# A fused attention and maxout kernel: new order of the work ahead of its main loop, eleven zero products in place of twenty-seven, and the next batch's scores ahead of the first product in each iteration

## The chip, the core and the metric

The kernel runs on one core of one Trainium2 chip. Such a core has four engines that compute, each with an instruction queue of its own: TensorE (PE in the profile; its weight loads are PEld), VectorE (DVE), ScalarE (ACT) and GpSimd (POOL). A fifth, SyncE (SP), here only issues data transfers. Products are accumulated in PSUM, which this kernel holds as eight named banks of 128 x 512 float32. The time of a run is the time of the whole execution on the device, in microseconds (us).

## The reference

For each of 8 batches and 8 heads, `x` (512 x 64) reads from a small `state` (32 x 64), and the state reads from `x`. The two results are put together to 4352 tokens of 512 numbers, which go through a maxout layer of two weight matrices and an output matrix:

```python
scores = scale * np.matmul(x, state.transpose(0, 1, 3, 2))
a = np.exp(scores - scores.max(-1, keepdims=True))
a /= a.sum(-1, keepdims=True) + 1e-09
xread = np.matmul(a, state)                      # (8, 8, 512, 64)
# sread: the same with x and state exchanged       (8, 8, 32, 64)
x2 = np.concatenate([xread, sread], axis=2)      # heads merged: (4352, 512)
h1, h2 = x2 @ w1, x2 @ w2                        # 512 x 1024 each
out = np.maximum(h1, h2) @ w_out                 # 1024 x 512
```

## The kernel before

**Algebra.** max(h1, h2) is written as relu(h1 - h2) + h2. So the weights needed are `wd` = w1 - w2 (the `sub` pieces) and `wwo` = w2 @ w_out (the `ww` pieces, from transposed w2 in `w2m` and from `wo`, the bfloat16 copy of w_out). Since xread = a @ state, each batch b first multiplies its state with these weights (`sw` pieces, into the tile `sw`), and layer one is then relu of the transposed attention weights `at` times `sw` (`l1`, evacuated by `re` into the tile `r`). The output product of `r` with `wo` is made by a seven-product scheme in place of eight (Strassen's, as Winograd has it): products 1 to 7 (`p1` to `p7`, line 426, 8 matmuls of 256 columns each), sums of `r` (`rs`, `r_sum`, into `big5`), sums of `wo` (`wt`, into `big3`), parts kept on the way (`k0` to `k2`), `wwo`'s share added with line 432 (`p2o`, `o7`, `o3`, `o4`), and results put into the output tile (`v00` to `v10`).

**Stages.** Ahead of the loop, batches 0 and 1 are worked through entirely and batch 2 up to its attention weights, while the weights arrive. A loop over batches b = 2 to 6 then does layer one and the output products of batch b together with the scores, exponentials and state products of batch n = b + 1. A tail finishes batch 7 and the 256 tokens of the state's readings.

**What sets the order.** A manual schedule is used: every engine runs its instructions in the order in which the program calls them, and waits on semaphores for what it reads. Ahead of the loop that order is the string `ORDER` (lines 23 to 48), a list of pieces. `sc.2.0@4` is the first half of the scores of batch 2, into bank 4; `xte.0.1>V` is the copy of a transposed half of `x`, on DVE (A is ACT, P is POOL); `ld...` pieces are loads on SP, in the order of the list. The pieces that the prediction names:

- `fill.k@r`: one product of zeros (tile `wz`, line 575), of 512 columns (256 where k is below 100). Nothing reads it.
- `ldw2.k`, `ldw1.k`, `ldwo.k`: quarters of the weights, 512 KB each; `ldx.b.g`: half of a batch's `x`, 512 KB. `cw2`, `cwo`: casts of weights to bfloat16; `sub.k.h`: w1 - w2.
- `ce`, `cb`: casts of `x`; `xt`, `xte`: transposed `x` by TensorE, and its copy from PSUM; `xtd`: the same as a transposing transfer (line 242, tile `xt`).
- `sc`, `exp`, `red`, `mul`, `at`, `ate`: scores, exponential, sums, normalisation, transposed attention weights; `srw`, `swre`, `srp`, `sr`: the state's reading.
- `mS` (line 222), then `Sd` (line 228): the states of batches 2 to 7 are masked into the tile `sb`, and one transposing transfer makes the tile `sbd` of it. Scores from batch 2 on read `sbd`.

SP issues transfers in order, and a transfer waits in SP's queue until what it reads is written. Loads go through one queue, and each waits for the landing of the eighth transfer ahead of it.

In the loop, DVE runs `r_sum` 0 and 1, then the sums and reciprocals (`red`) of both score halves, then `r_sum` 2; POOL multiplies (`mul`) behind each `red`.

Of the kernel before, what the change touches and what calls it, by code (L numbers as in the profile page):

```python
# [24 lines left out]
fill.9@0 ldw2.3 fill.111@1 ldwo.2 fill.0@0 fill.5@1 fill.101@0 ldw1.3 ce.0.1>A ce.0.0>V ldwo.3 xt.0.0@0 cS.0.2>V  # L25
ldw1.2 fill.106@1 xte.0.0>V fill.105@2 ce.0.3>P ce.0.2>A ldw2.1 S.0.2@1 xt.0.1@2 ldw2.0 Se.0.2.1>A Se.0.2.0>V sc.0.0@1
xte.0.1>V fill.13@0 ldwo.0 fill.6@3 ce.1.2>P exp.0.0>A fill.115@4 fill.108@3 sc.0.1@4 ce.1.3>V ldwo.1 red.0.0>V
exp.0.1>A xt.1.1@3 ce.1.0>A ce.1.1>P srw.0@4,1 xte.1.1>V ldw1.0 mul.0.0>P swre.0.0>A red.0.1>V sc.1.1@3 xt.1.0@2
cw2.2>P exp.1.1>A ldw1.1 fill.15@4 fill.107@0 xte.1.0>V fill.1@4 swre.0.1>A fill.2@3 fill.14@0 fill.3@4 fill.112@3
cw2.3>A red.1.1>V mul.0.1>P fill.102@4 fill.7@3 ldx.2.0 fill.4@2 mul.1.1>V w2.3@2 cwo.2>A w2.2@3 w2e.3>V sc.1.0@4  # L30
at.0.0@0 at.0.1@1 exp.1.0>A w2e.2>V ww.3.2@2 ldx.2.1 ww.2.2@4 red.1.0>V sub.3.1>P ate.0.0>A srw.1@3,5 ate.0.1>A
mul.1.0>V cwo.3>A ww.0.2@1 sub.3.0>V at.1.0@0 at.1.1@6 swre.1.0>A ww.1.2@7 sub.2.0>V ate.1.1>A ldS.2.8 ww.3.3@2
ww.1.3@7 sub.2.1>V ate.1.0>A ww.0.3@1 swre.1.1>A sw.1.1@0,6 sw.0.1@5,3 swe.1.1.0>A swe.1.1.1>V ww.2.3@4 swe.0.1.0>A
swe.0.1.1>V l1.1.5@6 cw2.1>P srp.0>P srp.1>P l1.1.7@0 cw2.0>A re.1.5>V l1.0.7@3 w2.1@5 re.1.7>V re.0.7>A w2.0@6 w2e.1>V cwo.0>A
l1.0.5@3 l1.1.6@0 w2e.0>V l1.1.4@5 cwo.1>A ww.2.0@4 re.0.5>V ww.1.0@7 re.1.4>A ww.2.1@4 sub.0.0>V ww.1.1@7 re.1.6>A
sub.0.1>V ww.3.0@2 wwe.2>A ww.0.1@1 sub.1.1>V ww.3.1@2 wwe.1>A ww.0.0@1 sub.1.0>V wwe.3>A l1.0.4@7 wwe.0>A cb.2.0>P
sw.0.0@2,4 re.0.4>V wt.0>P sw.1.0@0,5 swe.0.0.0>A swe.0.0.1>V sw.0.w@1,3 sw.1.w@7,6 cb.2.1>P swe.1.0.0>A swe.1.0.1>V xtd.2 wt.1>P
p2.1@2 l1.0.6@4 swe.0.w.0>A re.0.6>V l1.0.3@0 l1.0.2@5 swe.0.w.1>A re.0.3>V swe.1.w.0>V mS.1>A
l1.0.1@4 l1.0.0@1 p2.0@3 swe.1.w.1>V mS.0>A Sd dif.0>P re.0.2>V re.0.1>A re.0.0>A p2o.0
l1.1.0@7 l1.1.1@6 l1.1.2@0 l1.1.3@5 re.1.0>V re.1.1>A re.1.2>A rs.0.0>V rs.0.1>V re.1.3>A  # L40
p2o.1 ldx.4.1 ldx.3.0 ldx.4.0 ldx.3.1
p1.0@1 k0.0>A p1.1@4 rs.0.2>V wt.2>V v00.0 p6.0 rs.0.3>V k0.1>A k1.0>A p5.0@7 wt.3>V v00.1 rs.1.0>V k2.0>A
sc.2.0@6 exp.2.0>A sc.2.1@0 exp.2.1>A sw.2.0@5,3 red.2.0>V mul.2.0>P red.2.1>V swe.2.0.0>A swe.2.0.1>A ce.2.0>A ce.2.1>A ce.2.2>A ce.2.3>A
p7.0 o7.0 v11.0 rs.1.1>V mul.2.1>P p3.0 o3.0 rs.1.2>V atd.2 sw.2.w@6,2 swe.2.w.0>A v01.0 swe.2.w.1>A
# [13 lines left out]
def kernel(  # L58
# [216 lines left out]
    def red(b, hh):  # L275
        nc.vector.tensor_reduce(es_all[:, b, hh], e_view(e_s[b % 2], hh), axis=AXX, op=ALU.add)  # L276
        nc.vector.reciprocal(er_s[b % 2][:, hh], es_all[:, b, hh])  # L277
# [145 lines left out]
    def product(pv, lhs, rhs, first=False, cc=(0, 1)):  # L423
        for c in cc:
            for f in range(4):
                nc.tensor.matmul(pv[c], lhs[:, f, 128 * c:128 * c + 128], rhs[:, f, :],  # L426
                                 start=first and f == 0 and (c == 0 or pv.split), stop=False, skip_group_check=True)
# [474 lines left out]
```

## Time and profile before

| | |
|---|---|
| time, median of 3 runs (lowest to highest) | 144.81 us (144.69 to 145.2) |
| the profiled execution: time, span of the profile | 144.88 us, 143.1 us |
| granted TensorE clock, mean | 0.996 |
| first zero product to first product of the loop | 1.29 us to 52.56 us |
| the five iterations | 52.7 to 119.5 us |
| HBM read, written | 15.20 MB, 8.91 MB |

The span covers the program's own instructions; 1.78 us of the execution lie around it. Each line of a timeline is a run of like instructions on one engine: start, length, engine and line of the code, operation, tile written and tiles read, shape, and in brackets how long the engine was idle before it and what ended that. A line number is often that of a helper (L102 is every copy on ACT), so the tiles tell what it is.

### The profile page before, as it was taken

The page shows a single profiled execution, that of the slowest core. Times are in us where ns is not written, and L with a number is a line of the kernel's source. Part 1 is how long each engine was busy: PE and PEld are TensorE (multiplying, and loading weights), DVE is VectorE, ACT ScalarE, POOL GpSimd, SP SyncE. Part 2 cuts the span into 40 slices and gives each one's busy share as a digit, 9 for nine tenths or more (in the row PEclk, how much of TensorE's full clock was granted, in tenths as well). Part 3 has the DMA queues.
Part 4 walks back from the last instruction along what each step waited for, and adds up shares of the span by engine and source line. Part 5 has one row for each costly group of instructions (what it writes and reads, how often), then busy time and mean ns, then how long its engine had stood idle before and what let it go on. Part 6 is the DMA issues. An engine that isn't in the chain of part 4 may idle for free.

```text
span 143.1 us, 3680 instructions
## 1 busy us (share of the span) xinstructions
PE 134.7 (94%) x1448; PEld 95.4 (67%) x1458; DVE 108.3 (76%) x197; ACT 86.9 (61%) x168; POOL 72.1 (50%) x99
## 2 busy tenths in 40 slices
PE   6889989999999999999999999999999999999980
PEld 2467725456787776786778477747876786788860
DVE  3488959868999938997899799669948997847420
ACT  4367589895689535855682769086726855753220
POOL 4147326099009993399269908971990464200000
PEclk9999999999999999999999999999999999999998
DMA  3999999945997979949995999759137042502073
GB/s 112 342 366 392 384 386 386 343 83 93 196 343 230 286 180 249 236 42 293 242 386 109 212 355 195 160 213 211 35 65 293 2 58 82 234 5 73 9 248 119
DMA packets 36452, 29.50 MB, mean 206 GB/s; under 512 B 22608, under 2 KB 32336, under 8 KB 35536
## 3 DMA queue, kind: packets, MB, share of 16 engines
q1 hardware_dynamic: 36160, 29.10, 70.8%
q8 instruction: 12, 0.20, 0.6%
q10 hardware_dynamic: 272, 0.13, 0.3%
q14 instruction: 8, 0.07, 0.1%
HBM read 15.20 MB, written 8.91 MB: 169 GB/s over the span
## 4 chain that ended last, share of the span: by engine, by line
PE 83%; DMA 11%; ACT 1%; issue 1%; DVE 0%; SPq 0%; DVEq 0%
PE bank L426 36%; PE bank L375 19%; PE bank L432 10%; DMA big<-in_moe_w_out_dram 8%; PE bank L352 5%; DMA big<-in_x_dram 4%; PE bank L606 3%; PE bank L473 2%; PE bank L515 2%; PE bank L264 2%; PE bank L304 2%; PE bank L513 1%; ACT wo L102 1%; PE bank L548 1%; PE bank L336 0%
## 5 line engine op out<-in xcount | busy, mean ns | idle before, releaser
L102 ACT COPY big<-bank 128x512 f32<-128x512 f32 (+2 forms) x40 | 21.9, 551 | 16.6 <-PE bank L426 8.4
L280 POOL TENSOR_TENSOR a<-e,er 128x512 bf16<-128x512 bf16 x14 | 16.7, 1209 | 29.5 <-ACT e L272 18.0
L370 DVE TENSOR_SCALAR r<-bank 128x512 bf16<-128x512 f32 x32 | 21.9, 690 | 11.7 <-PE bank L375 10.6
L375 PE MATMUL bank<-at,sw 128*128 128x512 bf16 x120 | 29.1, 379 | 0.6 <-DVE sw L104 0.2
L426 PEld LDWEIGHTS <-big 128*128 128x128 bf16 x256 | 23.9, 98 | 6.3 <-DVE er L277 2.1
L426 PE MATMUL bank<-big,big 128*128 128x256 bf16 x192 | 23.1, 273 | 0.1
L102 ACT CAST sw<-bank 128x512 bf16<-128x512 f32 x36 | 20.1, 608 | 3.2 <-PE bank L352 3.2
L375 PEld LDWEIGHTS <-sw 128*128 128x128 bf16 x128 | 12.2, 98 | 13.5 <-ACT sw L102 0.5
L368 ACT ACTIVATE r<-bank 128x512 bf16<-128x512 f32 x32 | 18.3, 597 | 4.9 <-PE bank L375 4.7
L426 PEld LDWEIGHTS <-r 128*128 128x128 bf16 x192 | 18.2, 98 | 3.8 <-issue 0.5
L402 DVE TENSOR_TENSOR big<-bank,big 128x512 f32<-128x512 f32 (+1 forms) x25 | 16.4, 660 | 5.4 <-PE bank L432 5.4
L106 POOL CAST xe<-big 128x512 bf16<-128x512 f32 x23 | 16.5, 749 | 6.1 <-DMA big<-in_x_dram 6.1
L426 PE MATMUL bank<-wo,r 128*128 128x256 bf16 x128 | 16.3, 273 | 0.0
L102 ACT COPY sread_t<-bank 128x128 bf16<-128x128 bf16 x8 | 3.2, 472 | 18.7 <-PE bank L336 15.5
L106 POOL CAST xb<-big 128x1024 bf16<-128x1024 f32 x12 | 12.2, 1035 | 4.7 <-DMA big<-in_x_dram 4.7
L432 PE MATMUL bank<-sw,at 128*128 128x256 bf16 x96 | 14.4, 273 | 0.0
L432 PEld LDWEIGHTS <-at 128*128 128x128 bf16 x128 | 12.5, 98 | 1.7
L402 DVE TENSOR_TENSOR big<-r 128x1024 bf16<-128x1024 bf16 x16 | 12.6, 788 | 0.6
L276 DVE TENSOR_REDUCE sums<-e 128x16 f32<-128x512 bf16 x16 | 10.6, 660 | 0.3 <-ACT e L272 0.2
L272 ACT ACTIVATE e<-bank 128x512 bf16<-128x512 f32 x16 | 8.9, 601 | 1.3 <-PE bank L264 1.3
L402 POOL TENSOR_TENSOR big<-sw 128x512 bf16<-128x512 bf16 x8 | 9.2, 1151 | 0.9 <-POOL a L280 0.9
L104 DVE CAST sw<-bank 128x512 bf16<-128x512 f32 x12 | 7.9, 679 | 0.6 <-PE bank L352 0.6
(100 smaller groups left out, 188.7 us busy)
## 6 DMA issues: line engine op xcount, KB each, us to landing
big<-in_x_dram SPq DMA_DIRECT2D x14, 512.0 KB, 6.2
out_dram<-big SPq DMA_DIRECT2D x7, 1024.0 KB, 5.3
big<-in_moe_w_dram SPq DMA_DIRECT2D x8, 512.0 KB, 12.0
big<-in_moe_w_out_dram SPq DMA_DIRECT2D x4, 512.0 KB, 11.6
big<-in_x_dram SPq DMA_DIRECT2D x1, 1024.0 KB, 6.9
out_dram<-big SPq DMA_DIRECT2D x4, 256.0 KB, 2.6
sf<-in_state_dram SPq DMA_DIRECT2D x1, 384.0 KB, 10.4
out_dram<-w2m SPq DMA_DIRECT2D x2, 128.0 KB, 2.5
```

Source lines behind the costliest of these rows:

```text
L102: nc.scalar.copy(o, i)
L104: nc.vector.tensor_copy(o, i)
L106: nc.gpsimd.tensor_copy(o, i)
L272: nc.scalar.activation(out=e_view(e_s[b % 2], hh).rearrange("p (g c) i n -> p g c (i n)", g=2), in_=p.rearrange("p (c g m) -> p g c m", c= ...
L276: nc.vector.tensor_reduce(es_all[:, b, hh], e_view(e_s[b % 2], hh), axis=AXX, op=ALU.add)
L280: (nc.gpsimd if eng == "P" else nc.vector).tensor_mul(e_view(a_s[b % 2], hh), e_view(e_s[b % 2], hh), er_s[b % 2][:, hh].unsqueeze(3).to_b ...
L368: nc.scalar.activation(out=o, in_=p, func=ACTF.Relu)
L370: nc.vector.tensor_scalar(o, p, scalar1=0.0, scalar2=None, op0=ALU.max)
L375: nc.tensor.matmul(p, sw_s[b % 3][:, g, f * 128:(f + 1) * 128], at_s[b % 3][:, g].rearrange("p c t -> p (c t)"), start=(g == 0), stop=(g = ...
L402: (nc.gpsimd if eng == "P" else nc.vector).tensor_tensor(o, i0, i1, op=op)
L426: nc.tensor.matmul(pv[c], lhs[:, f, 128 * c:128 * c + 128], rhs[:, f, :], start=first and f == 0 and (c == 0 or pv.split), stop=False, ski ...
L432: nc.tensor.matmul(pv[c], at_s[b % 3][:, g, 2 * i + c, :], rhs[:, g, :], start=False, stop=False, skip_group_check=True)
```

## The change

`ORDER` is replaced. It has the same pieces, except that 11 `fill` pieces, all of 512 columns and all at the very start, stand in place of 27 (of 256 and 512 columns) that were spread over the first stage. The engines of many copies, the banks, and the order on every engine differ. In the loop, the scores of batch n and their exponentials now come ahead of the first product, and `red` and `mul` of the two halves come between the sums:

```diff
 ORDER = """
-ldx.0.0 ldS.0.2 fill.10@0 ldx.0.1 fill.109@1 ldx.1.1 fill.114@0 fill.11@1 ldx.1.0 fill.110@0 ldw2.2 fill.100@1
...
+fill.101@4 fill.102@1 fill.106@0 fill.107@2 fill.103@3 fill.108@2 fill.110@4 fill.109@3 fill.105@4 fill.104@3
+fill.100@7 ldx.0.0 ldS.0.2 ce.0.1>A cS.0.2>V ce.0.0>V ldx.0.1 ce.0.3>P ldx.1.1 ldx.1.0 ce.1.2>P ce.1.1>P ldw2.2 ldw2.3
...
         pX, pY, pZ = Pair(BX), Pair(BY), Pair(BZ)
+        pp = [sc_mm(n, hh) for hh in range(2)]
+        for hh in range(2):
+            sc_ev(pp[hh], n, hh)
         product(pX, rq(b, 0, 0), wq(0, 0), True)
         keep(0, pX, "A")
         r_sum(b, 0, "V")
+        red(n, 0)
+        mul(n, 0, "P")
         r_sum(b, 1, "V")
-        pp = [sc_mm(n, hh) for hh in range(2)]
-        for hh in range(2):
-            sc_ev(pp[hh], n, hh)
         product(pZ, rq(b, 0, 1), wq(1, 0), True)
         opened(b, pZ, 0, so_half(b, 0))
         pg = [sw_mm(n, 512 * z, 512 * z + 512, BY if z == 0 else "r") for z in range(3)]
         sw_ev(pg[0], n, 0, 512, 0, "A")
         sw_ev(pg[0], n, 0, 512, 1, "A")
-        for hh in range(2):
-            red(n, hh)
-            mul(n, hh, "P")
+        red(n, 1)
+        mul(n, 1, "P")
         at_dma(n)
```

Three places in the engines' queues matter below. Lines of the changed kernel are lower by three in these rows.

**TensorE, near the 256th instruction of its program.** Of the kernel before, six rows (`a` feeds the transposed attention weights, `wo,w2m` is a `ww` product):

```order
L291 LDWEIGHTS a_93
L291 MATMUL bank_64<-ident_71,a_93 128x128
L606 LDWEIGHTS w2m_80
L606 MATMUL bank_65<-wo_77,w2m_80 128x512
L606 LDWEIGHTS w2m_80
L606 MATMUL bank_67<-wo_77,w2m_80 128x512
```

Of the changed kernel, at the same count of instructions:

```order
L288 MATMUL bank_69<-ident_71,a_93 128x128
L288 LDWEIGHTS a_94
L288 MATMUL bank_68<-ident_71,a_94 128x128
L603 LDWEIGHTS w2m_80
L603 MATMUL bank_64<-wo_77,w2m_80 128x512
```

Before, the 257th instruction was the first load of `ww.3.2`, the first of the `ww` products. Now it lies inside the transposes `at.1.0`, which come behind three `ww` products, and 32 instructions of zero products less stand ahead of it.

**SP's queue, behind the last weights.** Before (`sf` is the state, `xt0` and `sbd0` the transposing transfers `xtd.2` and `Sd`, `big1` and `big9` hold `x` of batches 4 and 3):

```order
L192 DMA sf0_81<-in_state_dram 128x12x64
L242 DMA_TRANSPOSE xt0_87<-xb0_89 128x16x128
L228 DMA_TRANSPOSE sbd0_74<-sb0_82 128x12x128
L167 DMA big1_110<-in_x_dram 128x4x256
L167 DMA big9_118<-in_x_dram 128x4x256
```

And now:

```order
L189 DMA sf0_81<-in_state_dram 128x12x64
L164 DMA big1_110<-in_x_dram 128x4x256
L164 DMA big9_118<-in_x_dram 128x4x256
L239 DMA_TRANSPOSE xt0_87<-xb0_89 128x16x128
L225 DMA_TRANSPOSE sbd0_74<-sb0_82 128x12x128
```

Two loads of `x` went ahead of the two transposing transfers. One mask piece that `sbd0` waits for, `mS.0`, also stands elsewhere, in ACT's queue. Before, both mask pieces followed the copies of `sw`:

```order
L102 CAST sw0_102<-bank3_66 128x512
L222 ACTIVATE sb0_82<-sf0_81,mask0_83 128x12x64 x2
L368 ACTIVATE r0_105<-bank4_67 128x512
```

Now six copies of layer one stand between the last copy of `sw` and `mS.0` (`mS.1` is on DVE):

```order
L99 CAST sw1_103<-bank5_68 128x512
L365 ACTIVATE r0_105<-bank7_70 128x512
L365 ACTIVATE r0_105<-bank0_63 128x512
L365 ACTIVATE r0_105<-bank6_69 128x512
L365 ACTIVATE r0_105<-bank7_70 128x512
L365 ACTIVATE r0_105<-bank5_68 128x512
L365 ACTIVATE r1_106<-bank1_64 128x512
L219 ACTIVATE sb0_82<-sf0_81,mask0_83 128x12x64
```

**DVE in the loop's first iteration.** Before (`big5` receives `r_sum`, `e1` holds the exponentials):

```order
L402 TENSOR_TENSOR big5_114<-r0_105 128x1024
L402 TENSOR_TENSOR big5_114<-big5_114,r0_105 128x1024
L276 TENSOR_REDUCE sums0_79<-e1_92 128x16
L277 RECIPROCAL er1_96<-sums0_79 128x16
L276 TENSOR_REDUCE sums0_79<-e1_92 128x16
```

And now:

```order
L399 TENSOR_TENSOR big5_114<-r0_105 128x1024
L273 TENSOR_REDUCE sums0_79<-e1_92 128x16
L274 RECIPROCAL er1_96<-sums0_79 128x16
L399 TENSOR_TENSOR big5_114<-big5_114,r0_105 128x1024
L273 TENSOR_REDUCE sums0_79<-e1_92 128x16
```

The second sum, which the product behind the `sw` pieces reads, moved behind one sum of exponentials and its reciprocal.

More of the change, by code (lines that the diff above doesn't have):

```diff
@@ L23 @@
 ORDER = """
-ldx.0.0 ldS.0.2 fill.10@0 ldx.0.1 fill.109@1 ldx.1.1 fill.114@0 fill.11@1 ldx.1.0 fill.110@0 ldw2.2 fill.100@1
[L25 to L44, printed above, removed]
@@ new lines @@
+xte.0.1>V ldwo.0 sc.0.1@5 ldwo.1 exp.0.0>A exp.0.1>A ce.1.3>V xt.1.1@0 srw.0@2,3 ce.1.0>A red.0.0>V xt.1.0@5 xte.1.1>A
+sc.1.1@0 swre.0.1>A swre.0.0>A exp.1.1>A red.0.1>V mul.0.1>V xte.1.0>V ldw1.0 mul.0.0>P at.0.0@7 red.1.1>V ate.0.0>V
+sc.1.0@4 exp.1.0>A red.1.0>V mul.1.0>V ldw1.1 cw2.2>P w2.2@6 srw.1@1,5 swre.1.1>V cw2.3>P w2.3@2 w2e.3>V w2e.2>A
+swre.1.0>A sub.3.0>V sub.3.1>V ldx.2.0 cwo.2>P ww.0.2@1 ww.1.2@7 mul.1.1>P ww.2.2@4 at.0.1@6 at.1.0@5 cwo.3>A ww.0.3@1
+ate.0.1>A ate.1.0>A at.1.1@0 ate.1.1>A srp.0>A ww.1.3@7 cw2.1>P cw2.0>P ldx.2.1 ldS.2.8 sub.2.1>V ww.3.2@2 sub.2.0>V
@@ new lines @@
+sw.1.1@0,6 sw.0.1@5,3 swe.1.1.0>A swe.0.1.1>A ww.3.3@2 ww.2.3@4 swe.1.1.1>V l1.1.7@6 re.1.7>A swe.0.1.0>V l1.0.5@0
+l1.0.7@5 re.0.5>V re.0.7>A cwo.0>P l1.1.6@6 re.1.6>A w2.1@3 w2e.1>V cwo.1>V wt.0>V w2.0@0 w2e.0>A srp.1>A l1.1.4@6
+l1.1.5@3 re.1.5>A re.1.4>A ww.2.0@4 ww.3.0@2 ww.1.0@7 ww.1.1@7 wwe.1>A ww.2.1@4 wwe.2>A ww.0.0@1 ww.3.1@2 wwe.3>A
+ww.0.1@1 cb.2.0>P sub.0.1>V sub.0.0>V l1.0.4@6 wwe.0>A sub.1.0>V sub.1.1>V ldx.4.1 sw.0.0@2,4 sw.1.0@0,5 sw.0.w@1,3
+re.0.4>V swe.0.0.0>A sw.1.w@7,6 swe.1.w.0>V swe.0.w.0>V swe.1.w.1>V swe.0.w.1>V cb.2.1>V wt.1>V p2.1@2 swe.1.0.0>A
@@ new lines @@
+swe.0.0.1>A swe.1.0.1>A l1.0.3@7 l1.0.0@0 re.0.3>A l1.1.3@1 l1.0.6@6 re.0.0>A ldx.3.0 re.0.6>A l1.0.1@7 re.0.1>A
+l1.0.2@5 re.0.2>A dif.0>V mS.1>V rs.0.0>V rs.0.2>V rs.0.1>V wt.3>V p2.0@4 re.1.3>A mS.0>A p1.0@0 l1.1.0@5 p2o.0 p2o.1
+k0.0>A ce.2.0>A v00.0 l1.1.2@3 re.1.2>A l1.1.1@6 re.1.1>A p6.0 k1.0>A re.1.0>A xtd.2 Sd p5.0@1 sc.2.0@4 k2.0>A
+rs.1.0>V exp.2.0>A red.2.0>V wt.2>P rs.0.3>P p7.0 o7.0 sc.2.1@7 v11.0 exp.2.1>A red.2.1>V p1.1@4 p3.0 k0.1>A rs.1.1>V
+v00.1 p4.0 o4.0 o3.0 v01.0 rs.1.2>V rs.1.3>V ce.3.0>P ce.2.2>P ce.3.1>P mul.2.0>P ce.2.1>P ce.2.3>P mul.2.1>P cb.3.0>P
```

7 lines of the change are left out of this document (4 added, 3 removed).

## The prediction

> **What bounds the kernel now.** First the page's busy times and its chain of waits, by engine:
>
> ```profile
> PE 134.7 (94%) x1448; PEld 95.4 (67%) x1458; DVE 108.3 (76%) x197; ACT 86.9 (61%) x168; POOL 72.1 (50%) x99
> PE 83%; DMA 11%; ACT 1%; issue 1%; DVE 0%; SPq 0%; DVEq 0%
> ```
>
> TensorE ends last, behind a stretch of transfers. Where each holds is told by the table of windows (length, PE busy, granted clock, DMA share, GB/s):
>
> ```profile
> 6.00:16.00 10.00, 8.44 (x112) 1.00 1.05 376
> 18.90:29.10 10.20, 9.97 (x69) 1.00 1.08 364
> 29.10:40.70 11.60, 11.47 (x109) 1.00 0.73 144
> 40.70:52.70 12.00, 12.00 (x163) 1.00 0.82 252
> 66.10:79.60 13.50, 13.44 (x164) 1.00 0.87 248
> ```
>
> Up to 16 us the transfers are full and PE partly multiplies zeros. From 18.9 us on PE is full: idle are 0.23, 0.13 and nothing in the next three windows, 0.06 in an iteration. So an end can come earlier only if real products move into the time before 18.9 us, or if PE's dense stretch starts earlier; any new wait behind it is paid in full. In the loop there is nothing to win on PE.
>
> **Term 1, the weights' arrival.** What waits for weights, and PE's first products behind them (`sw` and layer one):
>
> ```profile
> 13.75 1.04 ACT L102 CAST wo<-big 128x1024 bf16<-128x1024 f32 x1 [0.30 <-DMA big<-in_moe_w_out_dram]
> 15.16 1.27 POOL L560 TENSOR_TENSOR wd<-big,big 128x512 bf16<-128x512 f32 x1 [1.73 <-DMA big<-in_moe_w_dram]
> 17.81 1.04 ACT L102 CAST wo<-big 128x1024 bf16<-128x1024 f32 x1 [1.41 <-DMA big<-in_moe_w_out_dram]
> 18.99 1.29 DVE L560 TENSOR_TENSOR wd<-big,big 128x512 bf16<-128x512 f32 x2 [1.22 <-DMA big<-in_moe_w_dram]
> 20.29 0.67 PE L352 MATMUL bank<-wd,sbd 64*32 64x512 bf16 x16
> 21.66 1.46 PE L375 MATMUL bank<-at,sw 128*128 128x512 bf16 x6 [0.17 <-DVE sw L104]
> ```
>
> Consecutive loads of 512 KB are used at 13.75, 15.16, 17.81 and 18.99 us: steps of 1.4, 2.65 and 1.2 where 524 KB at 386 GB/s need 1.36. `wo.3` came about 1.3 us late. One packet stands there that is no data:
>
> ```profile
> 0.00:15.50 15.50, 12.65 (x128) 8.40 (x130) 9.98 (x22) 8.76 (x16) 6.75 (x27) 1.00 0.90 309
> ...
> q8 instruction: 1, 0.02, 65.4%
> ...
> q8 instruction: 12, 0.20, 0.6%
> ```
>
> The first row counts 128 + 130 = 258 PE instructions up to 15.5 us; the second is queue 8 in the tenth of a microsecond behind; the last is that queue over the span: 12 packets for 2906 PE instructions, one in 242, 0.2 MB / 12 = 16 KB each. So I read it as the fetch of PE's next 256 instructions: one of the 16 DMA engines is taken for about a transfer's step, and the load that needs all sixteen lands late. The change takes 32 instructions out ahead of this place, so the 257th is reached in `at.1.0`, at about 17.5 us by the sums below, and `wo.3` should land at 15.1 + 1.36 = 16.45 and `w1.2` at 17.8 us. Loads behind stay 1.2 late as before.
>
> [...]
>
> **Term 2, PE up to the first `sw`.** The early stage itself is gated by the loads of `x`: both orders have the first reading products (`srw.0`) at about 10.1 us, since the same casts and exponentials lie ahead. From there DVE leads. Its pieces in the new order, by durations of like rows (copy of 1024 from PSUM 0.65, sums with reciprocal 0.9, `mul` 0.65): `red` twice, `mul`, `xte` from 9.6 to 12.7; `red`, `ate`, `red`, `mul`, `swre`, `w2e` 0.9 + 0.35 + 0.9 + 0.65 + 0.35 + 0.65 to 16.55. Only then can `ww.2.2` run; behind it PE has three `at` of 0.45 and four `ww` of 0.43: 16.6 + 3.1 = 19.7 us for the first `sw`, against 20.29. `wo.3`'s cast is done at 17.5, `w1.2`'s two `sub` at 17.85 + 1.3 = 19.15; both in time. With both `sw` (0.6) and two `ww` (0.86), layer one starts at 21.16, not 21.66: **0.5 us won**. Without term 1 the `sub` pieces end at 20.28 again and layer one starts at 21.75.
>
> The four copies of `srp.0` are now on ACT ahead of the copies of `sw`; The trace has them on POOL, and a like copy on ACT:
>
> ```profile
> 7.20 0.42 ACT L102 COPY sbd<-bank 64x128 bf16<-64x128 bf16 x2
> 21.45 2.60 POOL L106 COPY wz<-big 32x130 f32<-32x130 f32 x8
> ```
>
> Between 0.21 each (ACT's two) and 0.33 (POOL's eight) I take 0.21, the same engine's. That ends at 20.3, when the first `sw` is done; at 0.33 it costs 0.4 us of the gain.
>
> **Term 3, up to batch 2's scores.** From layer one's start to the next `sw` there are 7.35 us of products in both orders:
>
> ```profile
> 25.84 2.61 DVE L560 TENSOR_TENSOR wd<-big,big 128x512 bf16<-128x512 f32 x4 [0.28 <-DMA big<-in_moe_w_dram]
> 29.12 0.63 PE L352 MATMUL bank<-wd,sbd 64*32 64x512 bf16 x16
> 40.63 0.63 PE L264 MATMUL bank<-sbd,xt 128*128 128x64 bf16 x16
> ```
>
> PE would be there at 28.5; the last four `sub` end at 28.45 as before, with the last load. So 28.5 against 29.12: 0.6 won, and no more to be had. From 29.12 to the scores at 40.63 the old order takes 11.5 us, 0.13 of it idle; the new one has `p1.1` (8 matmuls, 0.87 by the chain) behind the scores. PE is ready for them at 28.5 + 11.5 - 0.13 - 0.87 = 39.0.
>
> But the scores read `sbd`, and its transfer starts later:
>
> ```profile
> 31.52 1.77 ACT L222 ACTIVATE sb<-sf,mask 128x768 bf16<-128x768 f32 x2
> 32.89 2.04 SPq L242 DMA_TRANSPOSE xt<-xb  x1
> 35.04 1.84 SPq L228 DMA_TRANSPOSE sbd<-sb  x1
> ...
> sbd<-sb SPq DMA_TRANSPOSE x1, 4.6
> at<-a SPq DMA_TRANSPOSE x6, 3.3
> ...
> DMA to landing us min/median/max: 4.2/5.3/9.9
> ```
>
> The rows of the DMA issues give the median from issue to landing; the last row is the same for `xtd`, line 242. Before, the mask was ready at 33.3 and `Sd` left as soon as SP had issued `xtd.2`: 35.04, landing 4.6 us later at 39.63, 1.0 us ahead of its use. Now `mS.0` stands behind six copies of layer one. PE ends the product of the fifth (`l1.0.2`) at 33.3, its copy ends at 34.2, the next at 34.7, `mS.0` (0.89) at 35.5. `Sd` leaves at 35.55 and lands between 39.3 (3.75, halfway between 8 blocks in 3.3 and 16 blocks in 4.2, the quickest `xt`) and 40.15 (4.6 again). I take 39.8. SP's two earlier loads of `x` wait for the `sub` pieces, leave at 28.5 and have landed by the time `xtd.2` goes at 33.1 (its DVE cast `cb.2.1` ends then), so they cost nothing; if `cb.2.1` were late, `xtd.2` would hold `Sd` behind it on SP. **PE's wait: 39.8 - 39.0 = 0.8 us (0.3 to 1.15)**, a stall that was not there.
>
> Behind it `p1.1` still has to run: 39.8 + 0.87 = 40.67, against 40.63. What was won by the arrival is spent: +0.04 us, from -0.46 to +0.4. From there to the loop the two orders hold the same products, and I find no wait in the new one: `red.2.0` ends at 41.8, `mul.2.1` on POOL at 45.8, so batch 2's weights land at 49, and the loop needs them at 52.6.
>
> **Term 4, the loop.** DVE and POOL of the second iteration, and PE's chain there:
>
> ```profile
> 70.44 0.69 DVE L402 TENSOR_TENSOR big<-r 128x1024 bf16<-128x1024 bf16 x1
> 71.17 0.69 DVE L402 TENSOR_TENSOR big<-big,r 128x1024 bf16<-128x1024 bf16 x1
> 71.78 0.68 DVE L276 TENSOR_REDUCE sums<-e 128x16 f32<-128x512 bf16 x1
> 72.56 0.25 DVE L277 RECIPROCAL er<-sums 128x16 f32<-128x16 f32 x1
> 73.63 0.91 DVE L402 TENSOR_TENSOR big<-r 128x1024 bf16<-128x1024 bf16 x1
> 72.95 2.50 POOL L280 TENSOR_TENSOR a<-e,er 128x512 bf16<-128x512 bf16 x2 [4.11 <-ACT e L272]
> 70.48 0.47 PE bank L264 x16
> 70.95 0.87 PE bank L426 x8
> 73.03 2.77 PE bank L426 x24
> ```
>
> On PE the two score halves only change places with product 1, 0.47 + 0.87 either way. On DVE the second sum now starts at 71.05 + 0.95 = 72.0 and ends at 72.7, or at 72.9 if POOL's `mul` beside it stretches it as it does the third sum (0.91 against 0.69). The product that reads it starts at 72.97. So the margin shrinks from 1.1 us to about 0.1, and I count a loss of 0.02 an iteration, 0.1 us in all (0 to 0.5). The transfer of the attention weights starts 0.5 us earlier, but nothing waits for it.
>
> **Zero products.** 16 fewer, off the path.
>
> ```profile
> 1.29 3.81 PE L575 MATMUL bank<-wz 128*128 128x256 bf16 x11 [1.29 <-DVE ones L578]
> ```
>
> These eleven had 6 x 512 + 5 x 256 = 4352 columns, 0.88 ns each. Eleven of 512 columns take 11 x 0.45 = 4.9 us, to about 6.2 instead of 5.1; the first transposes wait for a cast of `x` to 5.9 in any case, and the next half of `x` lands at 6.5.
>
> **Sum.** 0.04 + 0.1 = +0.1 us on 144.88 of the profiled execution (143.1 of span and 1.78 around it), which is 0.07 over the median of 144.81: 144.9 us.
>
> **Rivals.** *No stall at the scores* (144.1 us): `Sd` lands by 39.3, or ACT reaches `mS.0` earlier, and the loop's margin holds: 144.88 - 0.8, down to 143.9 if PE's early gain is larger than the 0.6. For it: the low end of the transposing transfers; against it: 4.6 in this very transfer. Chance 0.27. *The loop's second sum comes late* (146.1): it decides once that sum ends later than 72.9; each 0.25 us more (the stretch that two engines show beside each other is 0.22) is paid five times: +1.25. The other iterations have the same margins, so it would happen in all. Chance 0.12. *The order's model is wrong on fetches* (145.5): the fetch falls on `wo.3` or `w1.2` again, layer one starts at 21.75 and 0.6 us of term 2 and 3 are gone, with the stall kept. Chance 0.12. [...] No window of this trace shows a lower clock, so it gets 0.05. [...]
>
> The forecast keeps 0.44. A measurement here tells about 0.5%, 0.72 us, from no change, that is 144.09 and 145.53. Faster: 0.22 of the stall-free case and 0.05 of the forecast's low end, 0.27. Slower: 0.12 + 0.05, half of the fetch case and 0.02 of the rest, 0.25. Same: 0.48. The forecast's own range is 144.4 to 145.4; to hold 8 in 10 it reaches to 143.9 and 146.1.
>
> **What would show it.** The changed trace should have `wo.3`'s cast near 16.5 us, a PE wait of 0.3 to 1.15 us for a transfer ahead of the first L261 product near 40 us, and iterations of 13.3 us. Wrong would be: that cast still at 17.8, a PE stall in each iteration ahead of the product that reads the second sum, or long PE gaps with doubled matmul times before 16 us.

## The result, and the profile after

| | before | changed |
|---|---|---|
| time, median (lowest to highest) of 13 runs each | 144.99 us (144.69 to 145.82) | 146.2 us (145.48 to 160.25) |
| profiled execution: time, span | 144.88, 143.1 us | 146.0, 144.2 us |
| first loop product | 52.56 us | 52.78 us |
| iterations, start to start | 13.44, 13.49, 13.30, 13.30, 13.25 us | 13.94, 14.05, 13.22, 13.22, 13.25 us |
| last iteration's end to the end of the span | 23.8 us | 23.8 us |

Changed over before is 1.0071, interval [1.0052, 1.0091] (disturbed runs, the one of 160.25 us here and three of 176 to 485 us in two experiments below, are in no ratio). The change is slower by 0.7%; the forecast was no measurable difference. The spans differ by 1.12 us, and the table says where: 0.22 us ahead of the loop, 0.50 and 0.56 in the first two iterations, less 0.08 in each of the next two.

The page's busy times and its chain of waits by engine, of the changed kernel:

```profile
PE 133.9 (93%) x1442; PEld 93.8 (65%) x1442; DVE 105.0 (73%) x193; ACT 88.6 (61%) x176; POOL 75.0 (52%) x95
PE 74%; DMA 14%; DVE 6%; ACT 1%; SPq 1%; issue 1%; DVEq 0%
```

DVE's share of the chain was 0% and is 6%; the transfers' went from 11% to 14%. The table of windows (length, PE, PEld, DVE, ACT and POOL busy, granted clock, DMA share, GB/s) puts the idle time of PE in its place:

```profile
18.90:29.10 10.20, 9.68 (x70) 4.38 (x68) 7.63 (x12) 8.89 (x21) 3.63 (x4) 1.00 1.08 364
29.10:40.70 11.60, 11.12 (x110) 7.33 (x109) 8.82 (x15) 10.53 (x20) 6.14 (x6) 1.00 0.88 200
40.70:52.80 12.10, 12.10 (x162) 9.96 (x161) 9.79 (x17) 6.43 (x12) 11.38 (x14) 1.00 0.68 206
52.78:66.72 13.94, 13.45 (x165) 9.45 (x162) 11.80 (x22) 8.07 (x15) 9.34 (x11) 1.00 0.89 213
66.72:80.76 14.04, 13.45 (x164) 9.50 (x163) 12.18 (x23) 8.53 (x17) 9.49 (x11) 1.00 0.76 219
80.76:93.99 13.23, 13.23 (x164) 9.53 (x162) 10.60 (x20) 8.53 (x17) 8.69 (x10) 1.00 0.79 221
```

PE is idle for 0.52 us near the first `sw`, 0.48 near batch 2's scores, and 0.49 and 0.59 in the first two iterations; from the third on it is full. What PE waited for is in its list of waits (total, times, longest); of it:

```profile
PE bank L333 <- DVE sr L309: 1.1, 2, 0.6
PE bank L349 <- DVE wd L557: 0.5, 1, 0.5
PE bank L261 <- DMA sbd<-sb: 0.5, 1, 0.5
```

The first of these is not in my prediction. L333 transposes `sr`, a batch's state reading, and L309 on DVE scales that reading. In the first two iterations DVE scales two readings: the new one, out of a PSUM bank, and an old one made ahead of the loop, out of the SBUF tile `wz` (`srd`). The first iteration of the kernel **before**, from the timelines of DVE, POOL and PE (start, length, what):

```profile
64.36 1.45 DVE L312 TENSOR_SCALAR sr<-wz,sums 128x64 bf16<-128x64 f32 x2
...
61.91 2.74 POOL L106 CAST xe<-big 128x512 bf16<-128x512 f32 x4
64.62 1.15 POOL L402 TENSOR_TENSOR big<-sw 128x512 bf16<-128x512 bf16 x1
...
65.87 0.29 PE L336 MATMUL bank<-ident,sr 128*128 128x128 bf16 x2
```

The two scalings of the first row apart, in the view of the tile `sr` (shortest, median and longest of them in ns, first and last start):

```profile
L312 DVE TENSOR_SCALAR sr<-wz,sums x2: 341/770/1198, 64.4 to 64.6; 128x64 bf16<-128x64 f32 x2
```

And the timelines of the **changed** kernel, with the two scalings out of PSUM ahead of them:

```profile
63.93 0.47 DVE L309 TENSOR_SCALAR sr<-bank,sums 128x64 bf16<-128x64 f32 x2
...
61.66 2.74 POOL L103 CAST xe<-big 128x512 bf16<-128x512 f32 x4
64.36 1.15 POOL L399 TENSOR_TENSOR big<-sw 128x512 bf16<-128x512 bf16 x1
...
64.52 2.02 DVE L309 TENSOR_SCALAR sr<-wz,sums 128x64 bf16<-128x64 f32 x2
...
65.46 1.03 POOL L103 CAST xb<-big 128x1024 bf16<-128x1024 f32 x1
66.60 0.28 PE L333 MATMUL bank<-ident,sr 128*128 128x128 bf16 x2 [0.49 <-DVE sr L309]
```

The view of the tile there:

```profile
L309 DVE TENSOR_SCALAR sr<-wz,sums x2: 1044/1052/1059, 64.5 to 65.5; 128x64 bf16<-128x64 f32 x2
```

Equal pieces of 128x64 take 0.34 us or 1.04 to 1.20. What differs is the POOL operation beside them. Before, the first piece started under the last of POOL's short casts (`xe<-big`) and ended at 64.70, 0.05 us behind that cast's end at 64.65. The second started with POOL's difference (`big<-sw`) and ended at 65.82, 0.05 us behind its end at 65.76. In the changed kernel POOL's difference starts 0.16 us ahead of the first piece. That piece now ends at 65.56, behind the difference's end at 65.51, and the second at 66.54, behind the end of POOL's next cast, of 1.03 us, at 66.49. So the pair stands one POOL operation further on: beside difference and long cast, and no longer beside short cast and difference.

Measured from the iteration's first product, DVE's pieces start where they did (11.74 us, 11.80 before), but POOL's difference starts 0.48 us earlier (11.58, 12.06 before), since the new loop gives POOL its first `mul` earlier (6.17 us, 6.90 before). So an engine got ahead in its own work, and the product that had no slack (before, PE's transposes started 0.05 us behind the scaling's end) came half a microsecond late. From the third iteration on (b = 4) the program has no old reading to scale; the third and fourth iterations are 0.08 us *shorter* than before, the fifth is the same.

### The profile page after: what moved, and what is told of

Its sections match the earlier page's. It is cut to its first block, busy times and chain, and to the rows that moved or that the text cites. A ratio compares the mean times of both kernels' runs of the same rounds, so it can differ in the third digit from the quotient of the medians.

```text
span 144.2 us, 3664 instructions
## 1 busy us (share of the span) xinstructions
PE 133.9 (93%) x1442; PEld 93.8 (65%) x1442; DVE 105.0 (73%) x193; ACT 88.6 (61%) x176; POOL 75.0 (52%) x95
## 4 chain that ended last, share of the span: by engine, by line
PE 74%; DMA 14%; DVE 6%; ACT 1%; SPq 1%; issue 1%; DVEq 0%
PE bank L423 31%; PE bank L372 18%; DMA big<-in_moe_w_dram 8%; PE bank L429 8%; PE bank L349 5%; DVE sr L309 3%; DMA big<-in_x_dram 3%; PE bank L603 3%; DMA sbd<-sb 3%; PE bank L470 2%; PE bank L512 2%; PE bank L261 2%; PE bank L510 1%; PE bank L301 1%; DVE big L399 1%; DVE wd L557 1%
## 5 line engine op out<-in xcount | busy, mean ns | idle before, releaser
L277 POOL TENSOR_TENSOR a<-e,er 128x512 bf16<-128x512 bf16 x14 | 17.7, 1266 | 23.8 <-ACT big L99 17.7
L372 PE MATMUL bank<-at,sw 128*128 128x512 bf16 x128 | 29.8, 379 | 0.0
L99 ACT COPY big<-bank 128x512 f32<-128x512 f32 (+2 forms) x39 | 21.4, 555 | 12.0 <-PE bank L429 7.0
L367 DVE TENSOR_SCALAR r<-bank 128x512 bf16<-128x512 f32 x26 | 18.0, 692 | 11.3 <-PE bank L372 11.0
L365 ACT ACTIVATE r<-bank 128x512 bf16<-128x512 f32 x38 | 21.5, 598 | 4.5 <-PE bank L372 4.3
L103 POOL CAST xe<-big 128x512 bf16<-128x512 f32 x26 | 19.1, 769 | 6.0 <-DMA big<-in_x_dram 6.0
L399 DVE TENSOR_TENSOR big<-bank,big 128x512 f32<-128x512 f32 (+1 forms) x25 | 16.5, 662 | 7.7 <-PE bank L429 7.3
L423 PE MATMUL bank<-wo,r 128*128 128x256 bf16 x128 | 15.4, 272 | 0.0
L103 POOL CAST xb<-big 128x1024 bf16<-128x1024 f32 x11 | 11.2, 1038 | 4.6 <-DMA big<-in_x_dram 4.6
L399 DVE TENSOR_TENSOR big<-r 128x1024 bf16<-128x1024 bf16 x16 | 11.7, 737 | 2.5 <-ACT r L365 1.9
L399 POOL TENSOR_TENSOR big<-sw 128x512 bf16<-128x512 bf16 x7 | 8.1, 1152 | 1.3 <-issue 1.3
```

The lines of the kernel that those rows point to most:

```text
L99: nc.scalar.copy(o, i)
L103: nc.gpsimd.tensor_copy(o, i)
L277: (nc.gpsimd if eng == "P" else nc.vector).tensor_mul(e_view(a_s[b % 2], hh), e_view(e_s[b % 2], hh), er_s[b % 2][:, hh].unsqueeze(3).to_b ...
L365: nc.scalar.activation(out=o, in_=p, func=ACTF.Relu)
L367: nc.vector.tensor_scalar(o, p, scalar1=0.0, scalar2=None, op0=ALU.max)
L372: nc.tensor.matmul(p, sw_s[b % 3][:, g, f * 128:(f + 1) * 128], at_s[b % 3][:, g].rearrange("p c t -> p (c t)"), start=(g == 0), stop=(g = ...
```

## The experiments

All times below are beside runs of the kernel before on the same chip, and ratios are to those.

**The two halves of the change apart.** First the new table with the old loop; against the changed kernel its edit is

```diff
         pX, pY, pZ = Pair(BX), Pair(BY), Pair(BZ)
-        pp = [sc_mm(n, hh) for hh in range(2)]
-        for hh in range(2):
-            sc_ev(pp[hh], n, hh)
         product(pX, rq(b, 0, 0), wq(0, 0), True)
...
         r_sum(b, 1, "V")
+        pp = [sc_mm(n, hh) for hh in range(2)]
+        for hh in range(2):
+            sc_ev(pp[hh], n, hh)
```

and the `red` and `mul` of both halves behind the first copies of `sw`, as before.

> The new order of the pieces ahead of the loop, with the loop as it was before. Theory A (the loss is in the loop: in its first two iterations VectorE's scaling of the state readings of batches 0 and 1, which reads SBUF, is blocked by GpSimd's difference and cast of x, because the moved scores bring GpSimd ahead by some 0.3 us): those iterations go back from 13.9 and 14.05 us to 13.45, the pair of scaled pieces takes 1.2 to 1.5 us in place of 2.04, and the time is 144.9 to 145.2, with 0.2 us left to the order. Theory B (the new order ahead of the loop sets the phase of GpSimd, and the blocking comes from there): the two iterations stay at 13.9 or more and the time stays at 146.0.

Measured: 147.09 us, ratio 1.0130 [1.0104, 1.0156]; slower than both halves together, and more than either theory has. Then the new loop with the old table; against the changed kernel:

```diff
 ORDER = """
-fill.101@4 fill.102@1 fill.106@0 fill.107@2 fill.103@3 fill.108@2 fill.110@4 fill.109@3 fill.105@4 fill.104@3
...
+ldx.0.0 ldS.0.2 fill.10@0 ldx.0.1 fill.109@1 ldx.1.1 fill.114@0 fill.11@1 ldx.1.0 fill.110@0 ldw2.2 fill.100@1
...
```

> The order ahead of the loop as it was before, with the changed loop. Theory A: the first two iterations take 13.9 and 14.05 us and the time is 145.8 to 146.0, 0.9 to 1.1 over before. Theory B: 13.4 us an iteration and 144.7 to 145.0.

Measured: 145.85 us, ratio 1.0046 [1.0027, 1.0065], iterations of 13.95, 14.05, 13.22, 13.22 and 13.25 us. The old reading's scalings in its DVE timeline:

```profile
64.11 2.03 DVE L312 TENSOR_SCALAR sr<-wz,sums 128x64 bf16<-128x64 f32 x2
```

PE's list of waits from 30 us on has this one row:

```profile
PE bank L336 <- DVE sr L312: 1.1, 2, 0.6
```

So the loop's edit makes the two long iterations by itself. The run with the table alone has the old pair of durations (0.35 and 1.20 us) and yet a first iteration of 14.38 us, by another wait. SP's and PE's timelines there (`at` is the transposed attention weights):

```profile
61.84 1.23 SPq L282 DMA_TRANSPOSE at<-a  x1
...
66.78 1.46 PE L372 MATMUL bank<-at,sw 128*128 128x512 bf16 x5 [0.77 <-DMA at<-a]
```

That transfer took 4.9 us (61.84 to 66.74). A packet of instructions, of the kind of term 1, started at 64.71 us, while it was under way. In the fifth iteration the same happened (transfer from 116.37 to 120.87, packet at 118.66). In the changed kernel the transfer left at 61.73, had landed when the packet started at 64.96, and nobody waited. But in the kernel before, the same transfer had a packet inside it as well (62.41) and took only 3.6 us (61.99 to 65.58). Over the thirteen profiles of this document, 38 of 78 transfers of `at` have a packet started inside them: nine of these took 3.9 to 4.9 us, the other 29 took 3.0 to 3.6, and the 40 without a packet 3.0 to 3.7. So each of the longest transfers has a packet inside, but a packet does not make each transfer long, and that it is the cause is not shown. The profiled execution took 146.46 us, less than the median; where the rest was lost is not known.

**The scaling on ACT**, which takes it out of POOL's way and leaves the order of all other pieces as it is:

```diff
-            sr_ev(srd[:, b - 2], b - 2)
+            sr_ev(srd[:, b - 2], b - 2, "A")
...
+            if eng == "A":
+                nc.scalar.mul(sr_s[b % 2][:, g, :], p[:, 1 + 64 * g:65 + 64 * g], rr_all[:, b, g:g + 1])
```

> The changed kernel, but the scaling of the state readings of batches 0 and 1 (two pieces of 128x64 each, from SBUF) is on ScalarE, which idles for nearly 4 us there. Theory A: nothing waits for VectorE ahead of the two transposes, the first two iterations take 13.3 to 13.4 us, the time is 144.8 to 145.0, about 1.1 less than the changed kernel. Theory C (TensorE would have to wait there for something else that is late by the same, such as the put of a result into the output tile): the wait is renamed and the time stays within 0.3 of 146.0.

Measured: 144.9 us, ratio 0.9986 [0.9962, 1.0009]. The two scalings in ACT's timeline:

```profile
64.68 0.59 ACT L310 ACTIVATE sr<-wz,sums 128x64 bf16<-128x64 f32 x2 [1.54 <-DVE sums L307]
```

Its first two iterations in the table of windows:

```profile
52.86:66.22 13.36, 13.31 (x163) 9.50 (x162) 10.28 (x20) 8.65 (x17) 8.75 (x10) 1.00 0.94 214
66.22:79.50 13.28, 13.23 (x164) 9.57 (x163) 10.25 (x20) 9.12 (x19) 9.31 (x11) 1.00 0.78 228
```

The whole loss of the change is gone: ACT runs beside POOL's difference (64.45 to 65.60 there) and is not held up (0.35 and 0.33 us).

**Mask on POOL**: `mS.0` taken from behind ACT's six copies, for the stall at the scores.

```diff
-dif.0>V mS.1>V rs.0.0>V rs.0.2>V rs.0.1>V wt.3>V p2.0@4 re.1.3>A mS.0>A p1.0@0
+dif.0>V mS.1>V mS.0>P rs.0.0>V rs.0.2>V rs.0.1>V wt.3>V p2.0@4 re.1.3>A p1.0@0
```

> The changed kernel, but the mask piece mS.0 runs on GpSimd ahead of wt.2, where that engine idles, in place of ScalarE behind six copies of layer one. If the stall ahead of batch 2's scores is that piece's place, the transfer of sbd leaves at 35.9 in place of 36.4 and lands at 39.65, the wait of 0.45 us at 40.3 goes and the time is 0.4 less than the changed kernel's, 145.6. If the transfer's own latency sets it (it lands at 40.17 whenever it leaves a little earlier), the wait stays at 0.3 to 0.45 and the time at 145.9 to 146.0.

A miss: 147.31 us, ratio 1.0129 [1.0084, 1.0174]. POOL's and DVE's timelines, and PE's:

```profile
32.01 2.21 POOL L221 TENSOR_SCALAR sb<-sf,mask 128x768 bf16<-128x768 f32 x1 [1.95 <-DMA sf<-in_state_dram]
34.19 2.55 POOL L399 TENSOR_TENSOR big<-wo 128x1024 bf16<-128x1024 bf16 x1
34.68 2.60 DVE L399 TENSOR_TENSOR big<-wo,big 128x1024 bf16<-128x1024 bf16 x1
...
40.01 1.92 PE L423 MATMUL bank<-big,big 128*128 128x256 bf16 x16 [1.45 <-DVE big L399]
```

The mask takes 2.21 us on POOL (0.94 on ACT). Behind it POOL's sum of weights ran to 36.73, and DVE's sum beside it, 0.68 us in the changed kernel, took 2.60: it ended at 37.28, 0.55 us behind POOL's. Such a sum takes 0.63 to 0.69 us with no POOL operation under way at its start, so it can have done little of its work before POOL was done. The mechanism of the loop is thus seen at another place, with two other operations. The other mask piece stands behind that sum on DVE, so `Sd` left at 38.21, 1.8 us later than in the changed kernel, and the loop began at 54.52, 1.7 us later.

**Nineteen zero products in place of eleven**, of about the same columns, to bring the 257th PE instruction 16 instructions earlier in the work:

```diff
-fill.101@4 fill.102@1 fill.106@0 fill.107@2 fill.103@3 fill.108@2 fill.110@4 fill.109@3 fill.105@4 fill.104@3
-fill.100@7 ldx.0.0 ldS.0.2
+fill.100@4 fill.101@1 fill.102@0 fill.0@2 fill.1@3 fill.2@2 fill.3@4 fill.4@3 fill.5@4 fill.6@3 fill.7@7 fill.8@2
+fill.9@3 fill.10@2 fill.11@4 fill.12@3 fill.13@4 fill.14@3 fill.15@7 ldx.0.0 ldS.0.2
```

> The changed kernel with the same 5632 columns of zeros at its start, but as 3 products of 512 and 16 of 256 columns: 19 in place of 11, 16 more instructions of TensorE and no other change. Theory F (each 256th instruction of TensorE fetches a packet of 16 KB that makes the load then in flight land 1.2 to 1.4 us late): the first packet goes from 16.6 to some 15.3 to 15.8 us, so wo.3 is the load with the long step (2.5 to 2.7 us behind w1.3, its cast at 17.8 to 18.2) and w1.2 comes 1.2 to 1.4 behind it. Theory G (the long step belongs to a certain load, by its place in the queue or its source): w1.2 keeps the long step, as in the changed kernel's profile. For the time F gives 0.2 to 0.5 more ahead of the loop; the later packets shift too and may add or take some tenths.

Measured: 146.44 us, ratio 1.0088 [1.006, 1.0117]. Inconclusive on the packet: it started at 16.65 us (16.60 in the changed kernel), so the edit did not move it, and the loads had already fallen back 0.6 us at 12 us; no load shows a step beside it. No other run moves the packet at will. The first `sw` was at 20.26, as in the changed kernel.

**POOL's casts moved to ACT in the first two iterations**, to leave the second scaling nothing to stand behind:

```diff
-                cast_b(b + 3, g, "P")
+                cast_b(b + 3, g, "A" if b < 4 else "P")
```

> The changed kernel, with VectorE's scaling left as it is, but GpSimd's two casts of x behind its difference (L103 into xb) run on ScalarE in the iterations of batches 2 and 3. If VectorE's piece is held up by whichever GpSimd instruction runs beside it, the first scaled piece still waits for the difference (about 1.04 us) and the second, which the cast held up, falls to about 0.3: the pair takes 1.3 to 1.4 in place of 2.04, ends before TensorE is there, and the iterations go back to 13.4, the time to 144.9 to 145.1. If the slow pieces are slow for another reason (their source or the PSUM banks), they stay at 1.04 each and the time at 146.0.

A miss too: 149.07 us, ratio 1.0267 [1.0245, 1.0288]. POOL and DVE of it:

```profile
64.48 1.15 POOL L399 TENSOR_TENSOR big<-sw 128x512 bf16<-128x512 bf16 x1
...
64.64 2.16 DVE L309 TENSOR_SCALAR sr<-wz,sums 128x64 bf16<-128x64 f32 x2
...
65.60 1.15 POOL L399 TENSOR_TENSOR sb<-wwo 128x512 bf16<-128x512 bf16 x1
```

POOL's next sum moved up into the place of the casts, and the second scaling ended behind that (66.80 and 66.75). The iterations took 14.08 and 14.18 us. That explains 0.3 of the 0.4 us by which the span (144.6) is longer than the changed kernel's. But all five runs also have 4.0 to 4.3 us outside the span, where the other kernels have about 1.8: 148.89 us of time at a span of 144.6. The profile doesn't cover that, and it stays open.

**Loop alone, scaling on ACT**, with the old table:

> The order ahead of the loop as it was before, the changed loop, and the scaling of the two early state readings on ScalarE. The loop edit by itself cost 0.8 us (145.85 against 145.04); without the block the first two iterations should take 13.3 each, 1.4 us less than with it: 144.5. If the new order ahead of the loop has any worth, this is slower than the same with the new order (144.9).

Measured: 144.59 us, ratio 0.9969 [0.9953, 0.9985]; iterations of 13.28, 13.28, 13.22, 13.23 and 13.25 us. This is faster than both kernels.

**Mask on DVE and scaling on ACT**, in the changed kernel, for the stall at the scores:

```diff
-dif.0>V mS.1>V rs.0.0>V rs.0.2>V rs.0.1>V wt.3>V p2.0@4 re.1.3>A mS.0>A p1.0@0
+dif.0>V mS.1>V mS.0>V rs.0.0>V rs.0.2>V rs.0.1>V wt.3>V p2.0@4 re.1.3>A p1.0@0
```

> The changed kernel with the scaling on ScalarE (144.9 by itself) and the mask piece mS.0 on VectorE behind mS.1, where GpSimd is idle. The transfer of sbd then leaves as soon as xtd.2 is issued, at 35.9 in place of 36.4, lands at 39.6, and the wait of 0.45 us ahead of batch 2's scores goes: 144.5. If the sums that VectorE makes behind it come too late for product 6, the wait is only moved there and the time stays at 144.9.

Measured: 145.01 us, ratio 1.0 [0.9979, 1.0022], the same as with the mask on ACT (0.9986 [0.9962, 1.0009]). SP and PE of it:

```profile
33.40 2.12 SPq L239 DMA_TRANSPOSE xt<-xb  x1
35.63 1.75 SPq L225 DMA_TRANSPOSE sbd<-sb  x1
...
40.07 0.39 PE L261 MATMUL bank<-sbd,xt 128*128 128x64 bf16 x8 [0.76 <-DMA sbd<-sb]
```

A miss: the wait did not go. The masks were ready at 35.24 and `Sd` left right behind the issue of `xtd.2`, 0.8 us earlier than in the changed kernel (36.42), but it landed at 39.94, only 0.23 us earlier (40.17). `xtd.2` landed at 38.40 here and at 38.41 there. PE, whose first `sw` was early here, was ready at 39.31 and waited 0.76 us. How long `Sd` takes goes with how soon it leaves behind `xtd.2`: 2.1 to 2.2 us behind it, as here and in the kernel before, 4.3 to 4.6 us in six profiles; 2.5 us or more behind it, as in the changed kernel, 3.7 to 3.8 us in the other seven. So most of an earlier start is lost again, and the mask's place is worth little. The profiled execution took 144.36 us, less than the median.

**The scaling still on DVE, but earlier**, behind the fourth sum, where POOL runs short casts:

```diff
         r_sum(b, 3, "V")
+        if b < 4:
+            sr_ev(srd[:, b - 2], b - 2)
...
         sr_ev(p, n)
-        if b < 4:
-            sr_ev(srd[:, b - 2], b - 2)
```

> The changed kernel with one edit: in the first two iterations the reciprocal and the two scalings of the old reading (tile wz into sr) stay on DVE but stand right behind the fourth sum, ahead of POOL's difference, at about 62.8 us instead of 64.3. POOL then runs casts of 0.69 us each beside them. Theory A (a DVE scaling from this tile ends only when the POOL operation beside it ends, and only its place in time makes it long): the two pieces take at most 0.7 us each, TensorE's wait of 0.5 to 0.6 us for sr is gone, both iterations take 13.3 us, and the time is 144.9 us (144.6 to 145.2). Rival B (the scaling itself got slow in the new loop, wherever it stands, or DVE as a whole is late): the pieces keep 1.05 us each, the sums behind them come late instead, and the time stays at 146.0 or more.

Measured: 145.14 us, ratio 0.9984 [0.9958, 1.0009]; the first two iterations take 13.28 us. POOL's and DVE's timelines:

```profile
61.69 2.75 POOL L103 CAST xe<-big 128x512 bf16<-128x512 f32 x4
...
62.95 0.97 DVE L309 TENSOR_SCALAR sr<-wz,sums 128x64 bf16<-128x64 f32 x2
```

The two pieces apart, in the view of the tile:

```profile
L309 DVE TENSOR_SCALAR sr<-wz,sums x2: 408/526/645, 63.0 to 63.3; 128x64 bf16<-128x64 f32 x2
```

The pieces end at 63.36 and 63.92, 0.05 us behind the ends of two of POOL's casts (63.31 and 63.87), as they end 0.05 behind POOL's longer operations elsewhere: in the nine profiles with this scaling on DVE, all 36 pieces do. The same pieces, on the same engine, cost what stands beside them. The rival, that the scaling became slow in the new loop wherever it stands, is out. By its ratio this version is as fast as the one on ACT (0.9986). Its profile has one long iteration left, the third, of 13.73 us, where PE waits again for `at` (0.35 us) with a packet of instructions (89.71) inside its transfer (88.47 to 93.06).

With the old table, the same edit:

> The old order ahead of the loop, the new loop, and the scaling on DVE behind the fourth sum. Theory A: as with the scaling on ACT under the old order, 144.6 us (144.3 to 144.9), iterations of 13.3 us. Rival B: the two long iterations of 13.95 and 14.05 us stay, 145.85 us.

Measured: 144.41 us, ratio 0.996 [0.9939, 0.998], the fastest of all. Its first two iterations:

```profile
52.51:65.79 13.28, 13.28 (x164) 9.59 (x162) 11.06 (x22) 8.07 (x15) 9.46 (x11) 1.00 0.94 202
65.79:79.07 13.28, 13.28 (x165) 9.57 (x163) 11.03 (x22) 8.53 (x17) 9.39 (x11) 1.00 0.89 251
```

PE has no idle time left there. Last, the kernel before with nothing but the scaling on ACT:

> The kernel before (old order, old loop) with one edit: the two scalings of the old reading run on ACT. In the kernel before the second of them took 1.20 us beside POOL's difference, and its first two iterations 13.44 and 13.49 us against 13.30 later. Theory A: 0.14 and 0.19 us of that go, 144.7 us, and what the new loop itself wins over the old one, once the scaling is out of the way, is the rest to the 144.59 us of the new loop with the scaling on ACT: 0.1 us, 0.02 to 0.05 an iteration (13.22 against 13.30 us in the later iterations, so perhaps 0.3). Rival C (the new loop won nothing, all of the gain of 0.4 us came from moving the scaling): 144.5 to 144.6 us here too.

Measured: 144.77 us, ratio 0.9988 [0.9967, 1.0008], iterations of 13.30, 13.36, 13.30, 13.30 and 13.25 us. This is no measurable gain; the new loop's iterations, freed in the same way, are shorter by 0.02 to 0.08 us, 0.25 in all five. In one table (ratios to the kernel before):

| | scaling on DVE beside the difference | on ACT | earlier on DVE |
|---|---|---|---|
| old table, old loop | 1 | 0.9988 | not run |
| old table, new loop | 1.0046 | 0.9969 | 0.996 |
| new table, old loop | 1.0130 | not run | not run |
| new table, new loop (the change) | 1.0071 | 0.9986 | 0.9984 |

In the new loop the scaling beside the difference costs 0.8% (0.0077 with the old table, 0.0085 with the new). The new table costs about 0.2% in the new loop (three columns agree, by 0.0025, 0.0017 and 0.0024, each with an interval of about 0.002 on either side), and 1.3% in the old loop, where the long transfers of `at` come in; the halves do not add up. What the new loop itself wins, once the scaling is out of the way, is 0.0019, within the noise of the ratios; the iterations of the two profiles say 0.25 us.

## Why the prediction was wrong, and where right

The forecast stood on a median before of 144.81 us; with the ratio of 1.0071 that gives 145.8 us. This lies outside the forecast's own 144.4 to 145.4, and inside 143.9 to 146.1 only because that range had been widened for rivals. Most of the loss, 0.90 of 1.12 us, comes from a wait that neither the forecast nor any rival has, so that the time lies there is luck. It is near the price of the rival on the loop's second sum (146.1), by another mechanism.

**Term 4, the loop: the step that failed.** I took +0.1 us from the margin of the second sum; the loop gave +0.90. The margin itself held: in the first iteration that sum ended at 59.35, and the product that reads it started at 59.75 without a wait. So the rival that I had priced at 1.25 us for all five iterations did not happen. What I left out is what the earlier `mul` does to POOL. I followed DVE's own order and asked who waits for DVE; I did not ask which DVE operation would then stand beside which POOL operation. The trace of before held the clue, two equal scalings of 0.34 and 1.20 us, and I read only the sums' 0.91 against 0.69 out of it, as a stretch of 0.22. That sum (73.63 to 74.54) ended 0.55 us behind a `mul` of POOL (73.99). The size of the stretch depends on how much of POOL's operation is left: 0.36 us at the start of this sum of 0.91, 2.05 at that of the sum of 2.60 in the run with the mask on POOL, and at the start of the scaling of 1.20 us all of POOL's difference, 1.15.

What the runs show is who waits and until when. The scaling out of `wz` ends 0.05 us behind the end of a POOL operation each time, the sum of two SBUF tiles in the run with the mask on POOL 0.55 us behind. The same scaling out of PSUM takes 0.27 to 0.29 us in all 24 pieces of the profiles of before and after, also where a POOL operation is under way from its start to its end (63.78 to 64.06 in the kernel before, beside POOL's cast of 63.48 to 64.09). POOL is held in the same way: its `mul` takes 1.05 us, but 1.30 to 1.50 where a DVE sum of two SBUF tiles is under way at its start (58.95 in the changed kernel, 0.90 us behind that sum's end at 59.35). Why the one has to wait for the other, and why not when the scaling reads PSUM, is not shown.

**Terms 1 and 2, the arrival.** Here the rival on the order's model of fetches came true in the main, and the forecast did not. From the timelines:

```profile
16.92 1.05 ACT L99 CAST wo<-big 128x1024 bf16<-128x1024 f32 x1 [1.55 <-DMA big<-in_moe_w_out_dram]
...
18.87 1.29 DVE L557 TENSOR_TENSOR wd<-big,big 128x512 bf16<-128x512 f32 x2 [0.92 <-DMA big<-in_moe_w_dram]
...
20.22 0.63 PE L349 MATMUL bank<-wd,sbd 64*32 64x512 bf16 x16 [0.52 <-DVE wd L557]
...
21.65 1.96 PE L372 MATMUL bank<-at,sw 128*128 128x512 bf16 x8
```

`wo.3` comes without a long step, as predicted (16.92 for 16.5, since the load ahead of it was already 0.4 us later than before; the packet now starts at 16.60 instead of 15.54). But I had placed the packet at 17.5, where PE *runs* the 257th instruction (in this trace, the 129th weight load at 17.59). It came 0.9 us sooner than that forecast, and the next load, `w1.2`, came late: used at 18.87, a step of 1.95 us where 1.36 is the rule, and not at 17.8. With that, the 0.5 us of term 2 were gone: layer one at 21.65, before 21.66, as the rival had it (21.75). Where the load behind `w1.2` took the long step instead, the term was right:

```profile
19.60 0.63 PE L349 MATMUL bank<-wd,sbd 64*32 64x512 bf16 x16
```

That is the run with the new table and the old loop (packet at 17.07, `w1.2` landed at 17.94, the next load 2.39 us behind it; 19.7 predicted), and the run with the mask on DVE has 19.55 (packet at 17.31). Where the packet lands is not settled by the table alone: seven kernels with the same first 250 PE instructions as the changed one, itself among them, have it between 16.55 and 17.31. In two other runs (scaling on ACT, nineteen zeros) the loads had already lost 0.5 us and more at 12 us, and the load behind the packet was 0.2 us late or on time. So the first `sw` varies between 19.55 and 20.67 with the new table, and I should have given this rival more than 0.12. That the packet makes a load late is read from where the long step stands; no run shows it by moving the packet, and no trace tells how many of the 16 DMA engines a load needs. The 256 instructions to a packet were my estimate, from the 258 up to the first packet and the mean of 242: from one packet to the next, PE started some 170 to 310 instructions in the kernel before and 150 to 330 in the changed one. Nor is much to be won by its place: the load behind `w1.2` lands at 20.14 to 20.67 in all thirteen profiles. Of the 0.6 us, the loop's start shows less: 52.41 and 52.54 us with the early `sw`, 52.78 to 52.97 without it (54.52 with the mask on POOL).

**Term 3, the stall at the scores** came, by the transfer I named, at 0.45 us, within my 0.3 to 1.15 (0.8 taken):

```profile
33.94 1.91 SPq L239 DMA_TRANSPOSE xt<-xb  x1
...
35.45 0.94 ACT L219 ACTIVATE sb<-sf,mask 128x768 bf16<-128x768 f32 x1
...
36.42 1.52 SPq L225 DMA_TRANSPOSE sbd<-sb  x1
...
40.30 0.39 PE L261 MATMUL bank<-sbd,xt 128*128 128x64 bf16 x8 [0.45 <-DMA sbd<-sb]
```

`mS.0` ended 0.9 us later than I had it (36.39 for 35.5): layer one started 0.5 us later, and the products from there to the next `sw` took 7.76 us (21.65 to 29.41), nearly all of them busy, where I had counted 7.35 for both orders. That count was wrong on both; the kernel before took 7.46. `Sd` landed at 40.17 (39.8 predicted) and PE was ready at 39.85 (39.0). The two errors, 0.4 and 0.85 us, partly cancel, so the size of the stall is in part luck. `xtd.2` left at 33.94 and not at 33.1, and what the mask's earlier end would save is mostly lost again in `Sd`'s own transfer, as the run with the mask on DVE shows.

**Smaller steps.** The four copies of `srp.0` on ACT took 1.22 us, 0.3 each, near the 0.33 that I had named as the upper end and not the 0.21 I took; at that price I had counted 0.4 us lost, but with `w1.2` late they cost less. The zeros ran for 4.66 us, to 5.95. A lower clock with fewer zeros, for which the forecast has 0.05 of its "slower", did not come, and that fewer zeros lower it is shown by no run: from 6 to 18.9 us PE was busy for 10.11 us, and for 10.71 before, and the granted clock was 1.00 in both, as in each of the windows above. In both profiles it is lower at the end alone, 0.51 from 141.9 us on before and from 142.1 us on in the changed kernel, where PE has no instruction left. The sum, corrected by what was measured: 144.88 + 0.22 ahead of the loop + 0.90 in it = 146.0, the changed kernel's profiled time.
